# Output parts added in DRAM by accumulating stores from GpSimd, in an attention and gated MLP kernel on one Trainium2 core

## The chip, the cores and the metric

The kernel runs on one core of one Trainium2 chip. Times are device microseconds (us) from the first to the last instruction of an execution on that core, with what lies around it. Smaller is better. The engines are named as the profile names them: PE (TensorE matmul), PEld (its weight load), DVE (VectorE), ACT (ScalarE), POOL (GpSimd) and SP (SyncE, which only issues DMAs here).

## What is computed

Attention over 4 batches, 8 heads, 768 positions and 64 columns a head, where each query sees the first 8 keys and the last 96, with a bias by distance; then a gated MLP over the 3072 tokens, without a nonlinearity:

```python
scores = scale * np.matmul(q, k.transpose(0, 1, 3, 2)) + bias
scores = np.where(keep, scores, -1000000000.0)
a = np.exp(scores - np.max(scores, axis=-1, keepdims=True))
a = a / (np.sum(a, axis=-1, keepdims=True) + 1e-09)
x = np.matmul(a, v)                 # then (tokens, 512)
out = (x @ w_a) * (x @ w_b) @ w_out # 512 -> 1536 -> 512
```

All inputs and the output are float32.

## The kernel before

**Tiling.** The 3072 tokens are cut into six units `u` of 512 tokens. The 1536 inner columns are cut into six pairs of blocks, called `fp`. Not all weights fit at once, so the MLP runs in 18 passes (`PASSES`): each takes one unit through the one to three `fp` whose weights stand in SBUF at that time (`STAYS`, `TURNS`). So a unit's output, 512 tokens by 512 columns, is a sum over several passes. Most products are made by a seven-product scheme for 2x2 block matrices, in which DVE and ACT form the sums of blocks (`forms`, `convert`, `project`, `seven`). Attention for units 1 to 5 runs between the products of the earlier passes (`attention`, `granule_ops`), and ends in the ninth pass; its transposed tiles go through DRAM.

**Numbers as two parts.** A float32 operand is split in a rounded high part and a rest, so each product takes three matmuls. The matmuls into `acc` (`back`, 512 columns) sum a pass in four PSUM banks; in the late passes `strong_back` sums four quarters of the unit in three banks, each product of 256 columns at L1680.

**What happens at the end of a pass.** Where the next pass belongs to another unit, the unit's sum leaves PSUM. In passes 0 to 9 this is `evict`: four tiles `o` of 128 x 512 from three SBUF buffers. When the unit has no part yet, the bank is copied to `o` (`copy`, on ACT or DVE) and stored to a DRAM tensor of its own (`part`). When it has one, the old part is loaded into `o` ahead of time, DVE adds the bank to it (L1854), and `o` is stored to a new part, or to `out` if the unit is done. In passes 10 to 16 `strong_back` does the same for the four quarters, with the add at L1708. The last pass (unit 2) loads its old part into the tile `X` (`start_end`) and adds there. In all there are 32 loads `o<-part`, 4 loads `X<-part`, 36 stores to `part`, 20 stores from `o` to `out` and 5 from `X`; all are issued by SP at L650 (`dma`), save one last store by ACT.

**The order.** Each step is an `Op` with what it reads and writes. `ORDER` is a written-out list of all 3286 steps, and `ON_SCALAR` lists those that run on ACT where ACT and DVE both could. `Schedule.order` walks the list and each engine gets its instructions in that sequence; an engine never passes a waiting instruction. POOL has little to do: the small `TENSOR_SCALAR` on the softmax sums `sm` (L1133), one for each unit and pair of heads.

```python
for index in ORDER:
    op = self.ops[index]
    ...
    op.engine = "act" if index in ON_SCALAR else "dve"
```

Of the kernel before, what the change touches and what calls it, by code (L numbers as in the profile page):

```python
# [615 lines left out]
class Fast:  # L616
# [30 lines left out]
    def dma(self, due, out, src, reads, writes, nbytes, late=0.0):  # L647
# [3 lines left out]
            reads,  # L651
            writes,
            late=late,
            dma=max(nbytes / 325.0, 340.0),
        )

    def copy(self, due, out, src, n, reads, writes, psum=False):
# [1745 lines left out]
```

## Time and profile before

| | |
|---|---|
| time, median of 3 runs | 683.17 us (681.0 to 683.5) |
| profiled execution: time | 682.1 us |
| profiled execution: span | 680.2 us |
| PE busy | 659.8 us, 97% |
| DVE busy | 628.9 us, 92% |
| ACT busy | 390.8 us, 57% |
| POOL busy | 10.9 us, 2% |
| moved by DMA | 160.65 MB |

Matmuls are pipelined: a 256-column matmul is listed with 282 ns, but the next one starts 119 ns later. So the busy share of PE does not tell whether PE is at its pace; the number of matmuls in a stretch does, where they have one shape. The profiled execution's time is 1.9 us more than its span, and it lies inside the range of the runs.

### The profile page before, as it was taken

What the parts mean: (1) busy time and instruction counts of PE and PEld (TensorE: products, weight loads), DVE (VectorE), ACT (ScalarE), POOL (GpSimd) and SP (SyncE); (2) the same over time, 40 slices, a digit from 0 to 9 for tenths busy, and PEclk for the clock granted to TensorE, in tenths of its full rate; (3) what the DMA queues carried; (4) which work ended last, traced back from release to release, by engine and by line L of the source; (5) the groups of instructions that cost most, each with busy time, mean ns of one, the idle gap of its engine ahead of it and who ended that gap; (6) DMA issues with size and microseconds to landing.
All of it is one profiled execution on the core that took longest, in us unless ns stands there. A gap on an engine that the chain in (4) does not pass through costs nothing.

```text
span 680.2 us, 17612 instructions
## 1 busy us (share of the span) xinstructions
PE 659.8 (97%) x6735; PEld 612.6 (90%) x6735; DVE 628.9 (92%) x1632; ACT 390.8 (57%) x1073; POOL 10.9 (2%) x32
## 2 busy tenths in 40 slices
PE   6989999999999999999999999999999999999996
PEld 5779887879997889998999999999999999999996
DVE  8999998999999899869887989899999999999885
ACT  8999675677785666435546546256565346443310
POOL 1000000000000000000000000000000000000000
PEclk9999999999999999999999999999999999999999
DMA  8889999899999999998788986863634653224413
GB/s 331 294 308 292 319 277 327 295 338 317 306 301 354 300 309 296 298 287 284 231 267 234 272 250 197 258 219 109 209 117 166 203 157 112 94 68 140 135 63 114
DMA packets 81871, 160.65 MB, mean 236 GB/s; under 512 B 8114, under 2 KB 36914, under 8 KB 80114
## 3 DMA queue, kind: packets, MB, share of 16 engines
q1 hardware_dynamic: 81490, 159.22, 73.2%
q8 instruction: 55, 0.90, 0.6%
q14 instruction: 38, 0.31, 0.1%
q10 hardware_dynamic: 288, 0.22, 0.1%
HBM read 106.71 MB, written 52.69 MB: 234 GB/s over the span
## 4 chain that ended last, share of the span: by engine, by line
PE 73%; DVE 9%; DMA 9%; ACT 5%; issue 2%; SPq 1%; POOL 0%; DVEq 0%; ACTq 0%; POOLq 0%
PE al L1428 23%; PE ga L1428 17%; PE acc L1620 11%; PE m_acc L1680 7%; PE m_psS L1680 3%; DMA py<-mir 2%; PE ps L1056 2%; ACT t L1040 2%; DMA mir<-tt 2%; DVE tt L1190 2%; PE ps_al L525 1%; PE m_psA L1680 1%; DMA X<-dx 1%; DMA wr<-wts 1%; DMA px<-mir 1%
## 5 line engine op out<-in xcount | busy, mean ns | idle before, releaser
L1620 PE MATMUL acc<-w_O,hh 128*128 128x512 f32 x320 | 113.5, 402 | 0.5 <-DVE hh L662 0.3
L1428 PE MATMUL al<-xf_T,w_S 128*128 128x256 f32 x720 | 95.8, 282 | 0.7 <-ACT s L660 0.7
L1040 ACT ACTIVATE t<-t,sm 128x168 f32<-128x168 f32 x192 | 81.9, 429 | 18.9 <-DVE sm L1024 18.5
L1428 PEld LDWEIGHTS al<-xf_T,w_S 128*128 128x128 f32 x720 | 90.4, 188 | 2.2 <-ACT s L660 1.1
L1620 PEld LDWEIGHTS acc<-w_O,hh 128*128 128x128 f32 x320 | 60.1, 188 | 14.1 <-DVE hh L662 0.7
L1620 PE MATMUL acc<-w_O,hl 128*128 128x512 f32 x160 | 63.1, 394 | 0.2 <-DVE hl L670 0.2
L660 ACT COPY s<-al 128x512 f32<-128x512 f32 x53 | 30.9, 583 | 38.4 <-PE al L1428 37.3
L1024 DVE CUSTOM_DVE_ANT_0 t<-ps,mask 128x168 f32<-128x168 f32 x160 | 47.9, 326 | 1.4 <-PE ps L1056 1.2
L1160 ACT ACTIVATE t<-t,sm 128x168 f32<-128x168 f32 x116 | 40.5, 425 | 14.0 <-DVE sm L1140 13.9
L1428 PE MATMUL ga<-xf_B,w_S 128*128 128x256 f32 x360 | 48.0, 282 | 0.2 <-DVE w_S L670 0.2
L1428 PE MATMUL al<-xf_B,w_A 128*128 128x256 f32 x360 | 47.7, 282 | 0.2 <-DVE sm L1024 0.2
L1428 PE MATMUL al<-xf_T,w_A 128*128 128x256 f32 x360 | 48.0, 282 | 0.0
L1428 PE MATMUL ga<-xf_T,w_S 128*128 128x256 f32 x360 | 47.9, 282 | 0.0
L1428 PE MATMUL ga<-xf_B,w_A 128*128 128x256 f32 x360 | 47.7, 282 | 0.0
L1428 PEld LDWEIGHTS al<-xf_B,w_A 128*128 128x128 f32 x360 | 45.8, 188 | 2.0 <-issue 0.6
L1539 DVE TENSOR_TENSOR s<-ga,s 128x512 f32<-128x512 f32 x60 | 41.0, 684 | 5.4 <-ACT t L1040 2.5
L1428 PEld LDWEIGHTS ga<-xf_B,w_S 128*128 128x128 f32 x360 | 45.1, 188 | 0.6 <-DVE w_S L670 0.4
L1428 PEld LDWEIGHTS ga<-xf_T,w_S 128*128 128x128 f32 x360 | 45.1, 188 | 0.4
L1428 PEld LDWEIGHTS al<-xf_T,w_A 128*128 128x128 f32 x360 | 45.1, 188 | 0.4
L1428 PEld LDWEIGHTS ga<-xf_B,w_A 128*128 128x128 f32 x360 | 45.1, 188 | 0.3
L1190 DVE STREAM_TRANSPOSE tt<-t 128x512 f32<-128x512 f32 x80 | 40.6, 552 | 3.5 <-ACT t L1160 3.2
L660 ACT COPY sa<-al 128x256 f32<-128x256 f32 x26 | 9.7, 372 | 54.1 <-PE al L1428 52.2
(391 smaller groups left out, 1533.0 us busy)
## 6 DMA issues: line engine op xcount, KB each, us to landing
wr<-wts SPq DMA_DIRECT2D x36, 512.0 KB, 5.8
mir<-tt SPq DMA_DIRECT2D x80, 192.0 KB, 4.1
vt<-vd SPq DMA_DIRECT2D x24, 512.0 KB, 6.3
qk<-qk SPq DMA_DIRECT2D x20, 576.0 KB, 6.5
X<-dx SPq DMA_DIRECT2D x11, 1024.0 KB, 6.1
wl_S<-dw_S SPq DMA_DIRECT2D x36, 256.0 KB, 3.4
part<-o SPq DMA_DIRECT2D x36, 256.0 KB, 4.0
px<-mir SPq DMA_DIRECT2D x20, 448.0 KB, 7.3
```

What stands on the lines that cost most here:

```text
L525: self.main.nc.tensor.matmul(self.banks[s][64 * h : 64 * h + 64, o : o + 64], self.vt[rows, v0 : v0 + 64], src[rows, 2 * s : 2 * s + 2, 2 ...
L660: self.nc.scalar.copy(out(), src())
L1024: lambda e: nc.vector.tensor_tensor_reduce(t[:, i, h], bank[:, c0 : c0 + KW], self.mask[pair][:, h, kind], -0.125, 3.0e38, ALU.add, ALU.mi ...
L1040: lambda e: nc.scalar.activation(t[:, i, h], t[:, i, h], AF.Exp, bias=sm[:, 0, j : j + 1], scale=-1.0, accum_out=sm[:, 1, j : j + 1],),
L1056: nc.tensor.matmul(bank[64 * s : 64 * s + 64, c0 + c : c0 + c + w], qk[rows, q0 + 64 * s : q0 + 64 * s + 64], qk[rows, k0 + k : k0 + k + w ...
L1160: nc.scalar.mul(flat()[:, j], flat()[:, j], sm[:, 3, j : j + 1])
L1190: nc.vector.transpose(dst[:, :, e0 : e0 + n], src[:, :, c0 : c0 + 32 * n].rearrange("p j (e k) -> p j e k", e=n),)
L1428: self.nc.tensor.matmul(bank[:, ab * HT : ab * HT + HT], w[:, a, (2 * ab + c) * P : (2 * ab + c) * P + P], x[:, b, c], start=first, stop=F ...
L1539: lambda e: nc.vector.tensor_tensor(s[:, :], bank[:, :], s[:, :], op=ALU.add),
L1620: self.nc.tensor.matmul(acc[i][:, :], a[:, rows], w[:, b], start=first and f == 0 and k == 0, stop=False, skip_group_check=True,)
L1680: self.nc.tensor.matmul(bank[:, c * HT : c * HT + HT], fa(k, c * P, c * P + P), fb(l), start=first, stop=False, skip_group_check=True,)
```

## The change

A unit's part now lies in the unit's own rows of `out`. Its first part is stored there plainly by SP, as before to `part`. Every later part is copied from PSUM to `o` and added to those rows by a store with `accum_op=ALU.add`, issued by GpSimd (`gather`); nothing is loaded. So 32 loads and 32 adds of DVE go, 32 copies (24 on ACT, 8 on DVE) and 32 accumulating stores on POOL come. The last pass still loads its part, now from `out`. The list `ORDER` is new from start to end (3254 steps), and so is `ON_SCALAR`; the planner's other numbers stay.

```diff
 ORDER = (
-    161, 0, 12, 17, 1, 11, 19, 15, 21, 2, 6, 5, 3, 13, 16, 18, 4, 24, 181, 26, 22, 28, 7, 171,
...
+    def gather(self, due, out, src, reads, writes, nbytes):
+        self.plan.op(
+            due,
+            lambda e: self.nc.gpsimd.dma_start(out(), src(), accum_op=ALU.add),
+            reads,
+            writes,
+            dma=nbytes / 325.0,
+        )
...
     def part_of(self, u, due):
-        d = self.dram([NH, P, 512], F32, f"part{u}_{due:.0f}")
-        return d
+        rows = self.out[u * T : u * T + T].rearrange("(a p) c -> a p c", p=P)
+        return self.plan.buf(None, None, F32, f"part{u}", f"part{u}", tile=rows)
...
-        new = None if last or end else self.part_of(u, due)
+        more = old is not None and not end
+        new = None if end else old if more else self.part_of(u, due)
+        if more:
+            old = None
...
-            self.dma(due + n * step, to, at, keys, writes, 512 * 4 * P)
+            (self.gather if more else self.dma)(due + n * step, to, at, keys, writes, 512 * 4 * P)
...
     def evict(self, u, due, acc, first, last, final):
-        new = None if last or final else self.part_of(u, due)
+        old = self.part.get(u)
+        into = not (first or final)
+        new = None if final else old if into else self.part_of(u, due)
...
-                self.plan.op(
-                    due,
-                    lambda e, i=i, o=o: self.nc.vector.tensor_tensor(
-                        o[:, :], acc[i][:, :], o[:, :], op=ALU.add
-                    ),
...
+            self.copy(
+                due, lambda o=o: o[:, :], lambda i=i: acc[i][:, :], 512, [acc[i]], [o], psum=True
+            )
+            (self.gather if into else self.dma)(
```

In the rows of instructions below, a name ends in a running number, and `[waits ...]` names the semaphores of other engines: `DMASW0` to `DMASW7` are those of the accumulating stores, in turn, `DMAHW` those of the DMAs from SP. Most lines of the changed kernel have a number 7 to 10 higher than before (L660 is L667, L1620 is L1627).

POOL, from the softmax of unit 3 to that of unit 5, before:

```order
L1133 TENSOR_SCALAR sm_2_3470<-sm_2_3470 128x8 [waits Activation_49]
L1133 TENSOR_SCALAR sm_3_3871<-sm_3_3871 128x8 [waits Activation_49]
L1133 TENSOR_SCALAR sm_0_4176<-sm_0_4176 128x8 [waits Activation_49,Pool_49]
L1133 TENSOR_SCALAR sm_1_4427<-sm_1_4427 128x8 [waits DVE_49,Activation_49,Pool_49]
L1133 TENSOR_SCALAR sm_2_4702<-sm_2_4702 128x8 [waits DVE_49,Activation_49]
```

and in the changed kernel, where `o_..._232684` are the four tiles with which unit 0 leaves PSUM for the last time (after pass 4) and `o_..._270431` those of unit 1 (after pass 5):

```order
L1140 TENSOR_SCALAR sm_3_3859<-sm_3_3859 128x8 [waits Activation_49,Pool_49]
L658 DMA out<-o_0_232684_4029 128x512 [waits DMAHW7_49,Activation_49]
L658 DMA out<-o_2_232684_4091 128x512 [waits DMAHW2_49,Activation_49]
L1140 TENSOR_SCALAR sm_0_4165<-sm_0_4165 128x8 [waits DVE_49,Activation_49,Pool_49]
L658 DMA out<-o_3_232684_4161 128x512 [waits DMAHW0_49]
L658 DMA out<-o_1_232684_4063 128x512 [waits DMAHW7_49]
L658 DMA out<-o_1_270431_4536 128x512 [waits DMAHW3_49,DVE_49]
L658 DMA out<-o_2_270431_4423 128x512 [waits DMAHW3_49,Activation_49]
L1140 TENSOR_SCALAR sm_1_4406<-sm_1_4406 128x8 [waits Activation_49,Pool_49]
L658 DMA out<-o_0_270431_4544 128x512 [waits DMAHW4_49,DVE_49]
L658 DMA out<-o_3_270431_4691 128x512 [waits DMAHW4_49,Activation_49]
L1140 TENSOR_SCALAR sm_2_4680<-sm_2_4680 128x8 [waits Activation_49,Pool_49]
```

Eight stores have come between five small softmax steps; the other 24 stand behind the last of these, alone.

ACT at the end of the last pass of unit 0, before; here the four adds of this evict are on DVE and ACT has none of them:

```order
L1040 ACTIVATE t3_3_3870,sm3_3_3871<-t3_3_3870,sm3_3_3871 128x168 [waits DVE_49]
L660 COPY s5_3_1_3993<-al5_3_3899 128x512 [waits PE_49]
L660 CAST xf2_T1_248008_3999<-xT1_2_248008_3952 128x512 [waits PE_49]
L1160 ACTIVATE t3_3_3870<-t3_3_3870,sm3_3_3871 128x168 [waits DVE_49,Activation_49]
L1160 ACTIVATE t3_3_3870<-t3_3_3870,sm3_3_3871 128x168 x7
L660 CAST xf2_B11_248008_4051<-X_61 128x512 [waits DMAHW3_49]
L660 COPY sa5_3_4066<-al5_3_3899 128x256 [waits DVE_49,PE_49]
L660 CAST xf2_T4_248008_4072<-xT4_2_248008_4070 128x512 [waits DVE_49]
```

and in the changed kernel (`acc3_0` to `acc3_3` are the four banks of the pass that ends, `al6` is a bank of the next pass):

```order
L667 COPY o0_0_232684_4029<-acc3_0_3167 128x512 [waits DMAHW3_49,PE_49]
L1167 ACTIVATE t3_3_3858<-t3_3_3858,sm3_3_3859 128x168 [waits DVE_49,Activation_49]
L1167 ACTIVATE t3_3_3858<-t3_3_3858,sm3_3_3859 128x168 x3
L667 COPY sa5_3_4049<-al5_3_3877 128x256 [waits PE_49]
L667 COPY o0_1_232684_4063<-acc3_1_3121 128x512 [waits DMAHW4_49,PE_49]
L667 CAST xf2_T4_248008_4070<-xT4_2_248008_4037 128x512
L667 COPY o0_2_232684_4091<-acc3_2_3210 128x512 [waits DMASW0_49,PE_49,Activation_49]
L667 COPY o0_3_232684_4161<-acc3_3_3218 128x512 [waits DMAHW4_49]
L1047 ACTIVATE t4_0_4164,sm4_0_4165<-t4_0_4164,sm4_0_4165 128x168 [waits DVE_49,Pool_49]
L667 COPY vt3_2_3912<-ps4_0_ga_4123 128x4x64 [waits DMAHW2_49,DMAHW1_49,DVE_49]
L667 COPY s6_4_0_4200<-al6_4_4183 128x512 [waits PE_49]
```

All four copies are on ACT now. With three buffers for four tiles, the copy to `o0_2` reuses the buffer of `o0_0`, and waits for the first accumulating store to land (`DMASW0`); the copy to `o0_3` and the copy out of the bank `al6` stand behind it.

## Rows read from the trace of the kernel before

**Rows 1.** The page's first part: busy us, share of the span, instructions.

```profile
PE 659.8 (97%) x6735; PEld 612.6 (90%) x6735; DVE 628.9 (92%) x1632; ACT 390.8 (57%) x1073; POOL 10.9 (2%) x32
```

**Rows 2.** Six stretches: length, busy us (instructions) of each engine, granted clock, DMA, GB/s.

```profile
0.00:120.00 120.00, 107.51 (x1340) 92.50 (x1341) 112.86 (x370) 97.87 (x300) 6.09 (x17) 1.00 0.93 305
120.00:242.00 122.00, 120.53 (x1223) 104.92 (x1221) 117.73 (x297) 85.85 (x227) 1.93 (x6) 1.00 0.96 316
242.00:300.00 58.00, 57.66 (x674) 53.26 (x675) 50.76 (x141) 31.51 (x99) 1.11 (x3) 1.00 0.95 296
300.00:440.00 140.00, 140.00 (x1530) 128.90 (x1529) 123.60 (x321) 72.66 (x216) 1.78 (x7) 1.00 0.83 253
440.00:660.00 220.00, 219.96 (x1857) 219.03 (x1856) 212.71 (x490) 101.35 (x230) 0.00 (x0) 1.00 0.43 139
660.00:680.20 20.20, 14.15 (x120) 13.95 (x118) 11.29 (x19) 1.51 (x3) 0.00 (x0) 0.95 0.33 107
```

**Rows 3.** What PE waited for, 0 to 242 us: us, times, longest.

```profile
PE pu L1242 <- ACT py L660: 2.9, 2, 2.1
PE bank L2230 <- DVE X L2227: 2.4, 1, 2.4
PE ps L1056 <- DMA qk<-qf: 1.7, 1, 1.7
...
```

**Rows 4.** The same view from 242 us to the end.

```profile
PE al L1428 <- ACT s L660: 0.7, 1, 0.7
```

**Rows 5.** Pieces of the chain that ended last: start us, us, what.

```profile
112.08 1.78 PE pa L525 x64
...
259.86 1.44 PE al L1428 x12
...
268.40 2.78 PE acc L1620 x12
```

**Rows 6.** Timeline of PE, one block of score matmuls: start us, us, what.

```profile
251.05 1.11 PE L1056 MATMUL ps<-qk 64*64 64x168 f32 x36
```

**Rows 7.** Groups of DVE by line: form, count, busy us, mean ns, idle before.

```profile
L1024 DVE CUSTOM_DVE_ANT_0 t<-ps,mask 128x168 f32<-128x168 f32 x160 | 47.9, 326 | 1.4 <-PE ps L1056 1.2
L670 DVE TENSOR_TENSOR h<-s 128x256 f32<-128x256 f32 x90 | 36.7, 418 | 0.4
L1708 DVE TENSOR_TENSOR o<-m_acc,o 128x512 f32<-128x512 f32 x27 | 18.3, 684 | 1.0 <-PE m_acc L1680 1.0
L1162 DVE TENSOR_TENSOR t<-t,sm 128x672 f32<-128x672 f32 x11 | 9.3, 851 | 0.4
L1854 DVE TENSOR_TENSOR o<-acc,o 128x512 f32<-128x512 f32 x12 | 8.1, 679 | 1.1 <-PE acc L1620 1.1
L662 DVE CAST xf_T<-xT 128x512 fp32r<-128x512 f32 x9 | 3.8, 421 | 0.0
L662 DVE COPY o<-acc 128x512 f32<-128x512 f32 x4 | 2.7, 686 | 0.3 <-PE acc L1620 0.3
```

**Rows 8.** Tile o: copies on ACT, ns min/median/max, first and last start.

```profile
L660 ACT COPY o<-acc x12: 563/584/594, 117.4 to 418.5; 128x512 f32<-128x512 f32 x12
```

**Rows 9.** DMAs issued from 245 to 300 us: count, KB, median us to landing.

```profile
o<-part SPq DMA_DIRECT2D x8, 256.0 KB, 5.4
...
out<-o SPq DMA_DIRECT2D x5, 256.0 KB, 5.1
...
part<-o SPq DMA_DIRECT2D x1, 256.0 KB, 8.0
```

**Rows 10.** The same view from 440 to 660 us.

```profile
o<-part SPq DMA_DIRECT2D x21, 256.0 KB, 2.8
part<-o SPq DMA_DIRECT2D x20, 256.0 KB, 3.1
```

**Rows 11.** Tile sm on POOL: ns min/median/max; below, who waited for it (us, times).

```profile
L1133 POOL TENSOR_SCALAR sm<-sm x24: 231/312/1030, 11.0 to 423.3; 128x8 f32<-128x8 f32 x24
...
  DVE sm L1140: 1.8, 2
```

More of the change, by code (lines that the diff above doesn't have):

```diff
@@ L1744, in leave @@
                 return
-            if last or end:
+            if end:
                 to = lambda: self.out[r0 : r0 + 2 * P, c0 : c0 + HT].rearrange("(a p) c -> p a c", p=P)
@@ L1837, in evict @@
             o = self.sbuf([P, 512], F32, "o", f"o{u}_{i}_{due:.0f}", 3)
-            if first:
-                self.copy(
-                    due, lambda o=o: o[:, :], lambda i=i: acc[i][:, :], 512, [acc[i]], [o], psum=True
-                )
-            else:
-                old = self.part[u]
-                self.dma(
-                    due - LEADS[4],
-                    lambda o=o: o[:, :],
-                    lambda i=i, old=old: old[i],
-                    [(old, (i, 0)), (old, (i, 1))],
-                    [o],
-                    512 * 4 * P,
-                )
-                self.plan.op(
-                    due,
-                    lambda e, i=i, o=o: self.nc.vector.tensor_tensor(
-                        o[:, :], acc[i][:, :], o[:, :], op=ALU.add
-                    ),
-                    [acc[i]],
-                    [o],
-                    dve=dve(512),
-                )
-            if last:
-                r = u * T + i * P
-                self.dma(
-                    due, lambda r=r: self.out[r : r + P], lambda o=o: o[:, :], [o], [], 512 * 4 * P
-                )
-            else:
-                self.dma(
-                    due,
-                    lambda i=i: new[i],
-                    lambda o=o: o[:, :],
-                    [o],
-                    [(new, (i, 0)), (new, (i, 1))],
-                    512 * 4 * P,
-                )
+            self.copy(
+                due, lambda o=o: o[:, :], lambda i=i: acc[i][:, :], 512, [acc[i]], [o], psum=True
+            )
+            (self.gather if into else self.dma)(
+                due,
+                lambda i=i: new[i],
+                lambda o=o: o[:, :],
+                [o],
+                [(new, (i, 0)), (new, (i, 1))],
+                512 * 4 * P,
+            )
         if new:
```

479 rows, old and new, of tables (ON_SCALAR, ORDER) are left out of this document.

## The prediction

> **What bounds the kernel now.** I read the busy shares first [rows 1]: PE 97%, DVE 92%, everything else far below. A busy PE is not yet a PE at its pace, so the next views are the stretches [rows 2] and the list of what PE waited for [rows 3, 4]. They cut the run in two. Up to 242 us PE waits in many small pieces for ACT, DVE and a DMA; the sixteen rows of that list, of which three are shown, add up to 13.3 us [rows 3], and PE is busy 107.5 of the first 120 us [rows 2]. DVE is at work 112.9 of 120 and 117.7 of 122 us there [rows 2]: this part goes at DVE's pace. After 242 us PE waits once, for 0.7 us [rows 4], and is busy 417.6 of 418 us up to 660 [rows 2]. That this is a full pace is shown by the chain: twelve matmuls of 256 columns take 1.44 us, 120 ns each, twelve of 512 take 2.78 us, 232 ns each [rows 5], and from 440 to 660 us 1857 matmuls, almost all of 256 columns, make 118 ns each [rows 2]. The granted clock is 1.00 throughout, its upper level of 2.4 GHz, and 0.95 only in the last stretch, when PE has run dry [rows 2]. The last 6 us are a tail of adds and stores that the change leaves as it is.
>
> So from 242 us on, work that DVE or the DMA queues are spared is work beside a full PE, and is worth nothing by itself. What can move the time is PE's waits before 242 us, and new waits after.
>
> **The change part by part.**
>
> *The loads.* 32 loads of 256 KB leave SP's queue. The first was issued at 251 us, behind the border, so each lies beside a full PE: 0. While DMA is 0.95 busy up to 300 us, the loads made room for no one that PE waited for [rows 2, 4]. Gone with them is the add's wait for its load; late next is the copy's wait for its buffer, below.
>
> *The adds.* 12 adds at L1854 of 679 ns and 20 of those at L1708 of 684 ns go: 21.8 us of DVE [rows 7]. 32 copies come: 8 on DVE of 686 ns, 5.5 us [rows 7], 24 on ACT of 584 ns, 14.0 us [rows 8]. The new list also moves other steps between the two. Counted by form over the whole program, DVE has 32 512-column two-input steps fewer, and more: 2 copies (686), 7 casts (421), 16 casts half as wide (at most 421), 4 multiplies at L1162 (851), 3 half copies (about 418) [rows 7]. That is 21.8 less 1.4, 2.9, 3.4 to 6.7, 3.4 and 1.3, so DVE does 6 to 9 us less. All adds stood after 242 us: 0 on the path. If PE were not full there, it would be up to these 9 us.
>
> *The new list before 242 us.* This part has no accumulating store and no missing load; only the order differs. I compare both orders at one step that both have, just behind the border: the first matmul that reads the second half of the output weights of `fp` 3 (`w3_O1`), whose last writer is a DVE instruction. Before it DVE has 4 more 512-column two-input steps (684), 2 more of 256 (418), 2 more masked steps of L1024 (326), 2 more at L1162 (851) and one copy less (686): 2.74 + 0.84 + 0.65 + 1.70 - 0.69 = 5.2 us [rows 7]; the other differences are small copies that cancel. PE has 36 more 256-column matmuls done by then, 36 x 120 ns = 4.3 us that it need not do later [rows 5]. If DVE sets the time of this step, the change is 5.2 - 4.3 = +0.9 us; if PE does, 0. I take +0.5, since the trace has both near their pace here. How well the new list fills DVE's own gaps (7.1 and 4.3 us idle in the two stretches) no order tells; see the second rival.
>
> *The accumulating stores.* 32 on POOL, which is busy 10.9 us in all [rows 1] and whose queue holds only the 24 small softmax steps [rows 11]. Eight stores stand among these; each softmax step behind a store is fed by activations that ACT runs after the copy that the store waits for, so nothing is held back. The cost is in landing. A copy into `o` that reuses a buffer waits for the store that empties it, and in the copy's queue PSUM copies wait behind it, for which PE waits. The tightest place is the end of unit 0. From the last matmul into `acc3_0` to the first of the next pass into the bank of `acc3_2`, PE has 24 matmuls of 256 columns (2.9 us), 21 of 512 (4.9), 24 score matmuls (24/36 of 1.11) and 32 value matmuls (32/64 of 1.78): 2.88 + 4.87 + 0.74 + 0.89 = 9.4 us [rows 5, 6]. Two copies of 0.58 us [rows 8] must fit, so the first store has 8.2 us from the end of the copy to landing, POOL's issue included. The next is the end of unit 1: 48 matmuls of 256 and 12 of 512 and the same attention block, 5.76 + 2.78 + 1.63 = 10.2 us, less a copy on DVE and one on ACT, 8.9 us. In the late passes, the closest pairs I find in the order leave 10 us and more.
>
> How long such a store takes, no row shows. It moves 256 KB and also has to read its target. The near ends are a plain store, 5.1 us in this stretch (5.4 a load, 8.0 the slowest row) and a load and a store one after the other, 10.5 [rows 9]; the far end is two of the slowest, 16.0. After 440 us it is 3.1 to 5.9 [rows 10], under the 10 us that it has. At 5.1 to 8.0 it costs nothing, at 10.5 it costs 2.3 + 1.6 = 3.9 us, at 16.0 7.8 + 7.1 = 14.9. I take no cost: one transfer that reads and writes as it goes is nearer to one store than to two in turn. A gain is excluded, since PE waits for no store now [rows 3, 4]. The page "DMA: Bandwidth & Descriptors" of the Trainium skill (section "Anatomy of one DMA — SWDGE (gpsimd) path") fits such a GpSimd-issued DMA as 2.0 us plus its bytes at 436 GB/s, an estimate of 2.6 us here without the accumulation; by that the cost is also nothing, and the sum stays.
>
> *The sum.* 682.1 (the profiled execution) + 0 + 0 + 0.5 + 0 = 682.6 us. The median of the runs stands 1.1 above the profiled time and the lowest run 1.1 below it; I take 683.0.
>
> **The rivals.**
>
> *A, slower: the landing takes PE's banks.* The place is the buffer of `o0_0`, and the point from which it decides is a landing of 8.2 us. DMA is 0.95 busy there [rows 2], which speaks for it, and the slowest plain store already took 8.0 [rows 9]; against it, a queue of its own does not stand behind SP's backlog. At 10.5 us it gives 683.0 + 3.9 = 686.9. For this rival speaks a rule of the Trainium skill, page "SBUF — State Buffer", section "SBUF: two separate sides": GpSimd writes the descriptors of its DMAs through a port that it shares with DVE, and cannot while DVE runs certain fast steps, such as copies and casts within SBUF, so the DMA starts late. The trace shows something like it: one softmax step on POOL took 1030 ns where the median is 312 [rows 11]; that is 0.7 us of the 8.2, and would not decide alone.
>
> *B, faster: the new list fills the waits before 242 us.* DVE is idle 11.4 us there, PE waits 13.3 [rows 2, 3]. For it: the start is where all loss is, and every row of the list is new. Against it: at the common step both orders have the same work ahead within a microsecond. Half of DVE's idle time is 5.7 us, so 683.0 - 5.7 = 677.3.
>
> *C, slower: DVE becomes the bound late.* From 440 to 660 us DVE is idle 7.3 of 220 us [rows 2], and 20 stores are issued there. If each held up DVE for POOL's longest step, 1.03 us [rows 11], it would be 20.6 us, against 7.3 idle and the 20 adds that go there less 4 copies that come on DVE, 13.7 - 2.7 = 11.0 [rows 7]: 20.6 - 7.3 - 11.0 = +2.3, so 685.3. Against it: in the whole run DVE waited 1.8 us for POOL's 24 steps, 1.03 us at most for one [rows 11].
>
> **How the numbers follow.** The forecast, same pace and no landing wait, has 0.45 (683.0, from 680 to 686); A 0.20 (686.9, up to 697.9); B 0.24 (677.3); C 0.06 (685.3); other ends of a wholly new order 0.05, slower. A measurement of this kernel tells about 0.5% from no change, 3.4 us, so "same" is 679.8 to 686.6. Faster is B: 0.24. Slower is A, half of C and the rest: 0.28. Same is the forecast and the other half of C: 0.48. The range reaches down to 676, a little beyond B, and up to 690, which is A with a landing of 12 us; I leave 0.08 below it and 0.10 above.
>
> **What would show it.** Right: after about 245 us PE has no row of waits over 1 us, DVE's total falls by 6 to 9 us, ACT's rises, no load `o<-part` is left, and the accumulating stores land within 8 us. A shows as ACT idle before a copy to `o` near 255 to 262 us with the DMA `out<-o` named, and PE waiting for ACT behind it. B shows as PE busy over 110 of the first 120 us. C shows as longer DVE steps while POOL issues. The forecast is wrong if PE waits anywhere late, or if the first 242 us of work end more than 3 us earlier or later than now.

## The result, and the profile after

The changed kernel takes 685.42 us (median of ten runs, 683.07 to 690.49); the kernel before, timed beside it, takes 681.45 (ten runs, 680.19 to 683.5). The ratio is 1.0062, with an interval of 1.0038 to 1.0086. Three later comparisons of the same kernel gave 1.0034, 1.0050 and 1.0058; the mean of the four is 1.0051, which is 3.5 us. So the time that came lies 2.4 us above the forecast of 683.0 and inside the range, but "the same" was wrong: the kernel is slower, by about half a per cent. The profiled execution took 685.42 us, its span is 683.6; before it was 682.1 and 680.2.

The page's first part and its queues, after (for the first line, compare [rows 1]; a queue's line has packets, MB and share of the 16 DMA engines):

```profile
PE 660.2 (97%) x6735; PEld 613.0 (90%) x6735; DVE 623.7 (91%) x1630; ACT 391.7 (57%) x1063; POOL 44.4 (7%) x64
...
q1 hardware_dynamic: 67154, 142.44, 66.4%
q0 software_dynamic: 7168, 8.39, 9.2%
```

PE's work is the same to 0.4 us, and DVE did give up 5.2 us. POOL's busy time quadrupled: each store costs it about a microsecond of issuing ((44.4 - 10.9) / 32). The 8.39 MB of the 32 stores are cut into 7168 packets.

The same stretches as in [rows 2] (length, then busy us and instructions of PE, PEld, DVE, ACT, POOL, then granted clock, DMA share, GB/s):

```profile
0.00:120.00 120.00, 107.13 (x1338) 92.16 (x1339) 110.78 (x364) 99.99 (x308) 5.54 (x17) 1.00 0.94 302
120.00:242.00 122.00, 119.49 (x1223) 105.19 (x1222) 119.53 (x302) 84.36 (x227) 1.40 (x5) 1.00 0.97 314
242.00:300.00 58.00, 56.78 (x668) 51.94 (x667) 49.24 (x131) 27.38 (x81) 4.41 (x7) 1.00 0.97 268
300.00:440.00 140.00, 139.80 (x1528) 128.75 (x1527) 120.22 (x316) 74.98 (x220) 5.58 (x11) 1.00 0.82 242
440.00:660.00 220.00, 219.68 (x1840) 217.84 (x1839) 210.35 (x497) 101.94 (x222) 23.12 (x21) 1.00 0.49 118
660.00:684.00 24.00, 17.33 (x147) 17.13 (x145) 13.54 (x25) 3.07 (x7) 4.37 (x4) 0.94 0.53 92
```

PE is no longer full in the third stretch (56.78 of 58 us, 57.66 before). From 440 to 660 us it does 17 instructions fewer than before, but that is no sign of a slower pace: this execution comes to 440 us later in its work, and `after_again`, a second profile of the same kernel (experiment 2), has 1855 in the same window. The DMA share there rose from 0.43 to 0.49 (0.47 and 0.48 in the other profiles of this kernel; 0.36 and 0.37 in the SP kernel below, whose stores are plain), though the loads are gone: 20 adding stores keep the DMA engines busy for longer than the loads and plain stores that they replace.

What PE waited for from 242 us to the end, after; before it was one wait for 0.7 us [rows 4]:

```profile
PE acc L1627 <- ACT o L667: 1.4, 2, 1.2
PE ga L1435 <- DVE s L1546: 0.2, 1, 0.2
```

The 1.2 us is the wait that rival A names. ACT's timeline shows it (start us, us, what; in brackets the idle time before, and what ended it):

```profile
268.69 0.62 ACT L667 CAST xf_T<-xT 128x512 fp32r<-128x512 f32 x1
275.27 1.08 ACT L667 COPY o<-acc 128x512 f32<-128x512 f32 x2 [5.96 <-DMA out<-o]
```

and so does the chain of work that ended last, from 265 us on (start us, us, what):

```profile
265.12 10.05 DMA out<-o
...
275.27 0.59 ACT o L667
...
275.90 1.66 PE acc L1627 x6
```

The store was issued at 265.12 us and landed 10.05 us later. The prediction gave it 8.2 us. ACT stood before its copy for 5.96 us, with the next copy behind it; PE lost 1.2 us of that. But 1.2 us are not 3.5, and the other three profiles of this kernel have less: their waits of PE for ACT's copies to `o` add up to 0.3, 0.7 and 0.8 us. Most of the loss is not in the list of waits at all.

To find it I compared traces of the same list of instructions. The matmuls then come in the same order, so the time between the starts of two numbered matmuls can be set side by side. Four profiles of the changed kernel stand here against two of a kernel (`sp_plain` and `sp_again`, below) that has the same list and the same transfers, with every one of the 32 stores a plain store on SP's queue:

| matmuls | about when, us | stores on GpSimd, adding: mean (lowest to highest) | all on SP, plain | difference |
|---|---|---|---|---|
| 1 to 2250 | 2 to 214 | 210.6 (209.58 to 211.50) | 210.2 | +0.4 |
| 2250 to 2500 | 214 to 235 | 22.26 (20.73 to 24.60) | 20.81 | +1.45 |
| 2750 to 3000 | 257 to 281, end of unit 0 | 23.34 (22.90 to 24.33) | 23.20 (22.93 and 23.46) | +0.14 |
| 3250 to 3500 | 304 to 326, end of unit 1 | 22.75 (22.49 to 23.05) | 22.25 | +0.50 |
| 3500 to 5500 | 326 to 529 | 202.99 | 202.99 | 0 |
| 5500 to 6000 | 529 to 590 | 60.31 (60.13 to 60.44) | 59.87 | +0.44 |
| 6000 to 6734 | 590 to 677 | 87.51 | 87.52 | 0 |
| last matmul to the end | | 6.53 (6.50 to 6.57) | 5.65 | +0.89 |

The stretches from 2500 to 2750 and from 3000 to 3250, left out of the table, differ by 0.02 us or less in the mean. From 304 us on, the means of stretches in which nothing differs agree to 0.02 us, and the ranges of the three that differ do not overlap: 0.50, 0.44 and 0.89 us are clear of the noise. The 0.14 us at the end of unit 0 are not, since the two columns overlap there; nor are the first 0.4 us. The 1.45 us at 214 to 235 us stand before the first adding store is issued.

### The profile page after: what moved, and what is told of

The parts are those of the page before. It is cut to its first block, busy times and chain, and to the rows that moved or that the text cites. A ratio compares the mean times of both kernels' runs of the same rounds, so it can differ in the third digit from the quotient of the medians.

```text
span 683.6 us, 17567 instructions
## 1 busy us (share of the span) xinstructions
PE 660.2 (97%) x6735; PEld 613.0 (90%) x6735; DVE 623.7 (91%) x1630; ACT 391.7 (57%) x1063; POOL 44.4 (7%) x64
## 3 DMA queue, kind: packets, MB, share of 16 engines
q0 software_dynamic: 7168, 8.39, 9.2%
## 4 chain that ended last, share of the span: by engine, by line
PE 50%; DVE 13%; DMA 8%; issue 4%; ACT 2%; POOL 0%; SPq 0%; DVEq 0%; ACTq 0%; POOLq 0%
PE al L1435 18%; PE ga L1435 13%; PE acc L1627 7%; PE m_acc L1690 5%; DMA out<-o 3%; PE m_psS L1690 2%; DMA dx<-vt 2%; DMA px<-mir 1%; DVE h L677 1%; DVE s L1546 1%; DMA dw_S<-wm 1%; PE m_psA L1690 1%; DMA wr<-wts 1%; PE ps L1063 1%; DVE tt L1197 1%
## 5 line engine op out<-in xcount | busy, mean ns | idle before, releaser
L1627 PE MATMUL acc<-w_O,hh 128*128 128x512 f32 x320 | 114.0, 401 | 2.5 <-ACT o L667 1.4
L1047 ACT ACTIVATE t<-t,sm 128x168 f32<-128x168 f32 x192 | 81.9, 429 | 12.2 <-DVE sm L1031 11.8
L1627 PEld LDWEIGHTS acc<-w_O,hh 128*128 128x128 f32 x320 | 60.1, 188 | 15.4 <-ACT o L667 1.7
L1627 PE MATMUL acc<-w_O,hl 128*128 128x512 f32 x160 | 63.0, 394 | 0.0
L667 ACT COPY s<-al 128x512 f32<-128x512 f32 x54 | 31.5, 584 | 40.2 <-PE al L1435 36.4
L658 POOL DMA_DIRECT2D out<-o x32 | 34.8, 1109 | 248.6 <-DVE o L1718 121.7
L1167 ACT ACTIVATE t<-t,sm 128x168 f32<-128x168 f32 x100 | 35.0, 424 | 13.5 <-DVE sm L1147 13.5
```

The costliest lines, as they stand in the source:

```text
L658: lambda e: self.nc.gpsimd.dma_start(out(), src(), accum_op=ALU.add),
L667: self.nc.scalar.copy(out(), src())
L1047: lambda e: nc.scalar.activation(t[:, i, h], t[:, i, h], AF.Exp, bias=sm[:, 0, j : j + 1], scale=-1.0, accum_out=sm[:, 1, j : j + 1],),
L1167: nc.scalar.mul(flat()[:, j], flat()[:, j], sm[:, 3, j : j + 1])
L1627: self.nc.tensor.matmul(acc[i][:, :], a[:, rows], w[:, b], start=first and f == 0 and k == 0, stop=False, skip_group_check=True,)
```

## The experiments

Unless something else is said, the edit is to the changed kernel. Ratios are to the kernel before, timed beside each run.

**1. Where the accumulation and GpSimd come in.** Two kernels keep the new list and all its transfers. One issues the 32 stores on GpSimd without adding; the other moves them to SP:

```diff
-            lambda e: self.nc.gpsimd.dma_start(out(), src(), accum_op=ALU.add),
+            lambda e: self.nc.gpsimd.dma_start(out(), src()),      # pool_plain
+            lambda e: self.nc.sync.dma_start(out(), src()),        # sp_plain, sp_again
```

> The changed kernel with its 32 accumulating stores as plain stores from the same queue (the addition in DRAM is left out, so the parts overwrite each other). Theory L, if it is the addition that is slow: the first store at the end of unit 0 lands in about 5 us, ACT's wait of 6 us and PE's waits of 1.2 and 0.2 us go: 684 us, ratio 1.004. Theory O, or if the GpSimd queue is slow whatever it carries: 685.4 us, ratio 1.006.

> The changed kernel with its 32 accumulating stores as plain stores in SP's queue at the same places of the list (the addition in DRAM is left out). Theory L: landing near the 5 us of the plain stores, no PE wait at the end of unit 0: 684 us or less, ratio 1.003 to 1.004; what pool_plain loses against this is the GpSimd queue. Theory O: 685.4 us, ratio 1.006.

Measured: `sp_plain` 682.22 us, 1.0004 (0.9984 to 1.0023), and the same kernel once more 1.0005 (0.9985 to 1.0025). `pool_plain` 684.11 us, 1.0043 (1.0020 to 1.0065). So the new list with its copies and without the loads costs nothing that can be measured, and the loss goes when the stores are plain and on SP. In these kernels the parts overwrite each other instead of being added. Dropping the addition alone does not return it. The queue lines of `pool_plain`:

```profile
q0 software_dynamic: 2560, 8.39, 3.4%
```

The same bytes take 2560 packets and a third of the DMA time that the adding stores took, 3.4% against 9.2%. The places agree with this in part. At the end of unit 1 `pool_plain` needs the 22.25 us of the SP kernel, so the +0.50 there belongs to the addition. From 529 to 590 us it needs 60.38, so that loss stays with GpSimd, whether its stores add or not. Its tail is 6.35, but its last output store lands as early as on SP, 4.1 us behind the start of the last matmul; what is longer stands behind that landing, and one profile does not tell why. So 0.5 of the 2.7 us by which `pool_plain` is slower than `sp_plain` (1.0043 less 1.0004) are placed. Its one profile, a long execution with a span of 688.0 us, has large losses before 242 us (near 82 us and from 214 to 235), which experiment 4 and the last of the points below take up.

> The changed kernel with all 32 accumulating stores as plain stores in SP's queue, once more (the addition in DRAM is left out). If the stores on GpSimd are the loss: 1.000 to 1.001 again, and few executions above 683.5 us. If the new list is the loss and the first result was luck: 1.003 to 1.005.

The repeat of the SP kernel was run beside a repeat of the changed kernel, and gave the second column of the table its second profile.

**2. The new kernel again.** Three times, for the spread and for profiles to average:

> The changed kernel once more, for a second look at where its 4 us go and as a control beside the next runs. Theory L (the landing of the accumulating stores): the first one, at the end of unit 0, takes about 10 us again, ACT stands about 6 us before the copy to o, PE waits 1 to 2 us there. Theory O (the new list alone): the same ratio of 1.006 to the kernel before, whatever the landing does; PE's loss is spread in small waits before 242 us and after 540 us.

> The changed kernel a third time, as the control beside the two others: 683.5 to 685.5 us, ratio 1.003 to 1.006; a third look at the landing of the first accumulating store (10.0 us in the first two looks) and at PE's wait for px and py near 82 us (1.8 and 0 us).

> The changed kernel as the control: 683.5 to 685.5 us, ratio 1.003 to 1.006.

1.0034 (1.0016 to 1.0052), 1.0050 (1.0024 to 1.0075), 1.0058 (1.0033 to 1.0083). The landing that decides at each of the two tight places is that of the first store there. Beside it stands the time of the stretch of 250 matmuls around it:

| profile | first store of unit 0: landing | matmuls 2750 to 3000 | first store of unit 1: landing | matmuls 3250 to 3500 |
|---|---|---|---|---|
| changed kernel | 10.05 | 24.33 | 8.81 | 22.49 |
| `after_again` | 7.59 | 22.93 | 8.88 | 22.59 |
| `after_third` | 8.04 | 22.90 | 9.34 | 23.05 |
| `after_fourth` | 8.89 | 23.19 | 9.16 | 22.88 |
| `pool_plain` | 6.23 | 22.91 | 7.90 | 22.25 |
| `sp_plain` | 9.01 | 23.46 | 5.08 | 22.25 |
| `sp_again` | 8.25 | 22.93 | 5.80 | 22.25 |

So the expectation's "10.0 us in the first two looks" holds for the first look alone; the second had 7.59. At the end of unit 0 the stretch grows with a landing over some 8.5 us, whatever the store is, and adding stores (7.6 to 10.05) are not shown to land later than plain ones on SP (8.25 and 9.01). At the end of unit 1 they are: 8.8 to 9.3 us against 7.90 and less, and from 8.55 us on each 0.1 us of landing costs PE 0.1 us.

**3. The list.** `old_order` has the list of before, with each add turned into a copy on ACT and the loads taken out; its stores add. `old_order_sp` is the same with plain stores on SP.

```diff
 ORDER = (
-    (the new list)
+    (the list of before, without its 32 loads; 24 of the copies on ACT)
```

> The accumulating stores and the copies, in the list of the kernel before: each copy stands where the add stood, each accumulating store where the store stood, the loads are left out; the same 24 copies are on ACT as in the changed kernel. Theory L: the stores land as late as in the changed kernel, ACT waits for a buffer of o at the end of unit 0 and PE behind it: 683 to 686 us, ratio 1.003 to 1.006. Theory O: without the new list nothing is lost: 681 to 682 us, ratio 0.999 to 1.001.

> The list of the kernel before, copies for adds, no loads, and all 32 stores plain in SP's queue (the addition in DRAM is left out). If the stores on GpSimd are the loss: the 1.0083 of the same list with accumulating stores falls to 0.999 to 1.001. If it is the copies on ACT in places made for adds on DVE: it stays at 1.004 or more.

Measured: 1.0083 (1.0053 to 1.0112) and 1.0034 (1.0022 to 1.0047). So with plain stores the old list costs 0.3% where the new one costs nothing: its places for adds are the wrong ones for copies. Against the kernel before, the stretch of matmuls 2750 to 3000 takes 24.65 instead of 23.25 us, and that of 6250 to 6500 30.91 instead of 29.72. The new order is therefore no side matter: it takes back what the copies cost. With adding stores the tail grows from 5.98 to 8.35 us. POOL's timeline at the end of `old_order` shows how (start us, us, what, idle before and what ended it):

```profile
667.53 1.22 POOL L659 DMA_DIRECT2D out<-o  x1 [6.88 <-DVE o L1719]
672.13 1.20 POOL L659 DMA_DIRECT2D out<-o  x1 [3.39 <-issue]
677.64 1.21 POOL L659 DMA_DIRECT2D out<-o  x1 [4.31 <-DVE X L1730]
```

The tiles of the first two were both ready by 667.1 us, but the second store leaves 4.6 us after the first. The third, whose tile was ready at 677.09, leaves 0.3 us after the landing of the second and lands at 682.97 us, 5.33 us after its issue and after the rest of the program; as a plain store on SP it takes 2.60 us.

**4. Is the loss in the first 120 us?** A profile of the changed kernel and that of `pool_plain` had a matmul waiting near 82 us for a load (`px`, `py`), and that suggested a theory: the early order, not the stores, costs the time.

> The changed kernel, but its first 1226 steps (up to about 190 us, where both lists have done the same steps but for two each) stand in the order and on the engines of the kernel before; from there on the new list. Theory E (the new list's start: a load of px and py that lands 8 to 11 us after its issue, for which PE waits 0 to 2.9 us near 82 us, longer in slow runs): the loss goes, 681 to 682.5 us, ratio 0.999 to 1.001. Theory G (the GpSimd queue of the stores, wherever they land): 683.5 to 684.5 us, ratio 1.003 to 1.005, as in the changed kernel.

> The mirror image: the kernel before, with its loads and adds and no accumulating store, but its first 1226 steps in the order and on the engines of the new list. Theory E: 683 to 684.5 us, ratio 1.002 to 1.005, with a PE wait near 82 us for a DMA. Theory G: 681 to 682 us, ratio 0.999 to 1.001.

`early_old` has the first 1226 of the list's 3254 steps in the order of before, `before_early_new` is the kernel before with its first 1226 steps in the new order. Measured: 1.0045 (1.0028 to 1.0062) and 1.0016 (0.9995 to 1.0037). The old start does not cure the new kernel, and the new start does not spoil the old one by an amount that can be told. The theory fell. A second attempt moved the load instead, ahead of two weight loads of 512 KB in SP's queue:

```diff
 (SP's queue)
-L698 DMA wr_3<-wts 128x512
-L698 DMA wr_4<-wts 128x512
 L648 DMA px<-mir_1 112x1024
 L648 DMA py<-mir_1 64x512 x2
+L698 DMA wr_3<-wts 128x512
+L698 DMA wr_4<-wts 128x512
```

> The changed kernel with one edit of the list: two 512 KB weight loads that stand in SP's queue just ahead of the loads of px and py (the first value matmul after 82 us waits for these, up to 2.9 us, and in the run with the longest wait the granted clock fell to 0.89 behind it) stand just behind them. Theory E (that wait is what sets the changed kernel's slow executions): px and py land 2 to 3 us sooner, the wait goes, 682 to 683 us, ratio 1.001 to 1.002, and few executions above 684. Theory G (the stores on GpSimd): as the changed kernel, 683.5 to 684.5 us.

> The changed kernel with the loads of px and py ahead of two weight loads, and all 32 stores plain in SP's queue (the addition in DRAM is left out). If both the list and the GpSimd stores cost: 0.997 to 1.000. If only the GpSimd stores cost: as the kernel with all stores on SP, 1.000 to 1.001. If only the list costs: 1.002, as with the accumulating stores.

Measured: 1.0021 (1.0005 to 1.0037) with the adding stores, 1.0015 (0.9993 to 1.0037) with all stores on SP. The first looked like a cure for half of the loss. The second shows no gain from the move when the stores are plain, and a later kernel with the same move (experiment 6) gained nothing by it. I don't count it as a cause.

What the wait does to the clock can be seen in `pool_plain`, in two stretches around 82 us:

```profile
80.00:85.00 5.00, 3.04 (x25) 2.83 (x23) 4.88 (x12) 4.04 (x9) 0.02 (x1) 1.00 1.01 284
85.00:100.00 15.00, 14.05 (x170) 12.31 (x171) 10.13 (x33) 9.85 (x31) 0.23 (x1) 0.89 0.83 257
```

PE was busy for 3.04 of 5 us, and in the 15 us after that the granted clock was 0.89: part of that time at the lower of its two levels, 1.2 GHz instead of 2.4. The 250 matmuls that hold the wait take 18.94 us there (15.53 and 16.22 in the SP kernel), and the next 250 take 24.82 (23.92 and 23.80). That may be the price of the lower clock, but it isn't shown: `loads_first_sp` has no such wait and a clock of 1.00 there, and takes 24.66.

**5. Which stores.** `sp_12` puts the 12 stores of the first passes on SP, plain, and leaves 20 adding stores late; `sp_late20` does the opposite.

```diff
-            (self.gather if into else self.dma)(
+            self.dma(                                              # sp_12
...
-            (self.gather if more else self.dma)(due + n * step, to, at, keys, writes, 512 * 4 * P)
+            self.dma(due + n * step, to, at, keys, writes, 512 * 4 * P)  # sp_late20
```

> The changed kernel with 12 of its 32 accumulating stores (those at the ends of units 0, 1 and 2, before 450 us, while DMA is busy) as plain stores in SP's queue (their addition is left out), the 20 late ones as they are. Theory E: 683.5 to 684.5 us, ratio 1.003 to 1.005, as the early list is the same. Theory G: where the loss is the landing under a busy DMA, 682 us and a ratio of 1.000 to 1.001, as with all 32 on SP; where it is the late stores, 683.5 to 684.5 us.

> The mirror of the kernel with 12 stores on SP: the 12 accumulating stores at the ends of units 0 to 2 stay, the 20 of the late passes are plain stores in SP's queue (their addition is left out). If the late stores carry the loss (they go out one at a time, each 0.3 us after the one before has landed, and the last one lands beside the last output stores): the tail behind the last matmul falls from 6.5 to 5.7 us, PE gains 0.3 to 0.5 us between 440 and 660 us, 682 to 683 us, ratio 1.001 to 1.002. If the landings at the ends of the units carry it: ACT's wait of up to 6 us and PE's of up to 1.2 us stay, 683.5 to 684.5 us, ratio 1.003 to 1.005.

Measured: 1.0034 (1.0018 to 1.0051) and 1.0050 (1.0031 to 1.0068). This doesn't add up to the 1.0051 of both together, so the ratios give no split. The stretches do better, at two places: `sp_12` has 22.25 at the end of unit 1, with its own 12 stores plain, and 60.29 from 529 to 590, where its adding stores are; `sp_late20` has 59.82 there, and 22.57 at the end of unit 1, where its stores add. Each place follows the stores that stand at it. This holds in the other kernels too: with the early stores adding, the end of unit 1 takes 22.36 to 23.13 us in all nine profiles that have the new list there, and 22.25 in the five with plain ones. The late stretch hangs on the list as well: under the old list of experiment 3 it takes 59.95 us with adding stores and 59.99 without. The tail does not follow the stores: 6.15 in `sp_12`, but 8.44 in `sp_late20`, whose late stores are plain; its last transfer landed at 681.73 us and its span ended at 686.0. I have one profile of it and no explanation. For the +1.45 before the first store see the points below.

**6. The one-at-a-time issue.** An adding store of the late passes (L1761) writes two blocks of 128 rows. In POOL's timeline of the changed kernel the last ones stand in a regular row:

```profile
649.72 1.19 POOL L658 DMA_DIRECT2D out<-o  x1 [10.59 <-DVE o L1718]
654.62 1.21 POOL L658 DMA_DIRECT2D out<-o  x1 [3.70 <-issue]
659.57 1.19 POOL L658 DMA_DIRECT2D out<-o  x1 [3.75 <-issue]
...
669.46 1.19 POOL L658 DMA_DIRECT2D out<-o  x1 [3.94 <-ACT o L667]
674.26 1.20 POOL L658 DMA_DIRECT2D out<-o  x1 [3.60 <-DVE X L1867]
```

and the view of the tile gives the landing of the one of 654.62 (ns of its issue, when, and us to landing):

```profile
L658 POOL DMA_DIRECT2D out<-o x1: 1209/1209/1209, 654.6 to 654.6; - x1
...
DMA to landing us min/median/max: 4.6/4.6/4.6
```

654.62 + 4.6 = 659.2, and the next is issued at 659.57: some 0.3 us after the landing, and so on down the row. In none of the four profiles of this kernel are two of these 20 stores under way together. The program has no such wait. The last store is held until 674.26 and lands at 678.97, among the final stores of the output; on SP the three last of these stores went out at 660.6 to 666.3 us (in `sp_again`, whose end comes 3 us sooner). To test whether the size of one store is what limits it, `halves` issues each as two of 128 rows:

```diff
+    def pieces(self, out, src):
+        if len(src.shape) < 3:
+            return [(out, src)]
+        return [(out[:, k], src[:, k]) for k in range(2)]
...
-            lambda e: self.nc.gpsimd.dma_start(out(), src(), accum_op=ALU.add),
+            lambda e: [
+                self.nc.gpsimd.dma_start(to, at, accum_op=ALU.add)
+                for to, at in self.pieces(out(), src())
+            ],
```

`halves_loads` has the moved loads of experiment 4 as well.

> The changed kernel with each of the 20 late accumulating stores cut into two (128 rows of 1 KB each, where one store had 256). If the size of a store keeps the next one from being issued: a second store goes out while the first is under way, the queue no longer falls 4.7 us per store behind, the tail behind the last matmul falls from 6.5 to 5.7 to 6.1 us, and PE's two stretches near 500 to 590 us lose 0.4 us; 682.5 to 685 us, ratio 1.002 to 1.004. If an accumulating store always waits for the one before it: tail 6.5 us or more, ratio 1.004 to 1.006.

> The same with the loads of px and py ahead of two weight loads, near 72 us. If both edits take away what they are meant to: 681.5 to 683 us, ratio 1.000 to 1.002, no slower than before. If not: 683 to 685 us, 1.002 to 1.005.

Measured: 683.78 us, 1.0030 (1.0014 to 1.0046), and 683.86, 1.0031 (1.0016 to 1.0046). POOL's timeline of `halves`:

```profile
648.62 2.66 POOL L664 DMA_DIRECT2D out<-o  x3 [10.00 <-DVE o L1726]
651.80 0.86 POOL L664 DMA_DIRECT2D out<-o  x1 [0.52 <-issue]
652.94 0.86 POOL L664 DMA_DIRECT2D out<-o  x1 [0.28 <-issue]
654.11 0.99 POOL L664 DMA_DIRECT2D out<-o  x1 [0.31 <-issue]
```

The row of 3.6 us gaps is gone: gaps are 0.3 to 0.5 us, and the tail falls from 6.53 to 5.96, by 0.6 of the 0.9 us. So the issue does depend on the size of a store. There is still a bound: the first three of this row leave together, the fourth leaves 0.31 us after the landing of the first (648.62 us + 2.87), and so on; of the 40 half stores never more than three are under way, and 11 leave 0.31 us after the landing of the third before them. The packets tell a likely reason:

```profile
q0 software_dynamic: 7488, 8.39, 9.4%
```

A half store has 144 packets and a whole one 272 (12 x 144 + 20 x 272 = 7168; 52 x 144 = 7488). Three halves are 432 packets and may go together, two whole ones would be 544 and do not. A bound on packets under way, somewhere between, would fit both kernels, and also `pool_plain`, whose stores have 80 each and leave three together; no run tests it.

The price turns up elsewhere. PE's waits from 500 to 660 us in `halves`:

```profile
PE ga L1443 <- ACT s L675: 0.9, 1, 0.9
PE ga L1443 <- DVE s L1554: 0.3, 1, 0.3
```

Two stores side by side near 550 us hold up a load of SP's, ACT's weights behind it, and PE; the stretch of matmuls 5500 to 6000 takes 61.14 us. On the clock `halves` stands below the mean of the changed kernel, but its interval reaches over the 1.0034 of `after_again`, so a gain isn't shown. A fourth buffer of `o` was not tried.

**7. The kernel before once more**, for a trace against which the stretches can be checked:

> The kernel before once more, unchanged: a second look at how far its stretches differ between two executions. All theories: 680 to 684 us; from 450 us on within 0.3 us of the first look, before that within 2 us.

682.34 us. After 450 us its stretches agree with those of the first trace to 0.3 us, with one exception of 0.8 us (matmuls 5250 to 5500, 30.81 against 29.99), which was not expected. A single stretch of one profile can thus be off by nearly a microsecond; the means of the table above, whose ranges don't overlap at 304 to 326 us, 529 to 590 us and in the tail, are safer.

No kernel of these beats the kernel before.

## Why the prediction was off, point by point

**Loads, adds, list: right.** The all-SP kernel has the new list, no loads and the copies, and takes 1.0004 and 1.0005 of the time before, 0.3 us; the sum had +0.5 for these. DVE fell by 5.2 us (628.9 to 623.7; 6 to 9 were forecast), ACT rose by 0.9, and neither moved the time. This fits the reason given, that from 242 us on PE is full and spared work is worth nothing: without its loads and adds the SP kernel is no faster. Experiment 3 adds what the prediction did not weigh: the same edit under the old list would have cost 0.3%.

**Rival B did not happen.** PE is busy 107.13 of the first 120 us, 107.51 before; B asked for over 110.

**The step that failed is the price of the adding stores: "I take no cost: one transfer that reads and writes as it goes is nearer to one store than to two in turn".** In its place the four comparisons showed 3.5 us, of which 0.5 us stand at the end of unit 1, 0.44 in the late passes and about 0.5 in the tail; the rest stays open. At the end of unit 1 the first adding store landed in 8.8 to 9.3 us, where plain ones took 7.90 on GpSimd and 5.1 to 5.8 on SP. The two ends worked out from [rows 9] were 5.1 us (one store) and 10.5 (a load and a store in turn): it is nearer to the upper one, which I had called the less likely. In the late passes it takes 4.4 us in the median (4.0 to 6.8, 80 stores in four profiles) for the same 256 KB, against 3.1 of a plain store and 5.9 of a load and a store in turn [rows 10]: halfway between. On this the Trainium skill, page "DMA: Bandwidth & Descriptors" (section "Anatomy of one DMA — SWDGE (gpsimd) path"), agrees for the store that does not add: its fit gives an estimate of 2.6 us, and the 20 late plain stores of `pool_plain` took 2.6 us in the median (2.5 to 5.8). The adding stores took 1.7 times that in the median of the late passes, and up to 3.9 times in the first profile at the end of unit 0 (10.05 us).

A second part of the error is the place itself: at the end of unit 0 even a plain store on SP took longer than the 5.1 us. The view of the tile in `sp_again`, at the same step:

```profile
L658 SPq DMA_DIRECT2D out<-o x1: 557/557/557, 264.9 to 264.9; - x1
...
  ACT o L667: 3.4, 1
DMA to landing us min/median/max: 8.3/8.3/8.3
```

8.3 us, with ACT waiting 3.4 us and PE not at all. Rival A was priced at 3.9 us for a landing of 10.5 at both places; 0.64 us came on the mean, 0.14 at unit 0, which is not clear of the noise, and 0.50 at unit 1. The budgets were fair: the forecast was 8.2 and 8.9 us, and by the table of experiment 2 the stretches begin to grow at some 8.5 us in both places. The landings are what lay lower, 7.6 to 10.05 us. So A named the right mechanism, but its sure place is the end of unit 1, and it is a seventh of the loss.

**The tail.** The prediction called it "a tail of adds and stores that the change leaves as it is". Against the kernel before that is nearly so: 6.36 and 6.27 us in its two profiles, 6.53 after. But the same list with plain stores on SP ends in 5.65, so what the list had won is lost. The prediction looked at the last stores only for their landing time (under the 10 us they have) and not for when they can be issued. They go out one at a time, the last one lands among the final stores of the output, and the last of these lands 4.45 to 4.79 us behind the start of the last matmul, where the SP kernel has 4.1; in `halves` it is 4.1 again. That is 0.5 of the 0.89 us. The other 0.4 us stand behind the last landing, a time that is 1.4 to 2.3 us in these kernels, with adding stores and without (4.3 in `sp_late20`), and I don't put it down to the stores.

**The late passes were called free, and cost 0.44 us.** The prediction weighed who waits for an adding store, and there it was right: no such wait is in PE's list. It did not weigh what the store's transfers do to others. Matmul by matmul the difference stands at two places: 0.04 to 0.34 us between numbers 5720 and 5740, and 0.14 between 5900 and 5920, where PE waits 0.2 us for DVE. DMA issues from 530 to 590 us, after:

```profile
out<-o POOLq DMA_DIRECT2D x8, 256.0 KB, 4.6
...
wl_A<-dw_A SPq DMA_DIRECT2D x4, 256.0 KB, 4.4
```

and with the same stores plain on SP (`sp_again`; the last number is the median us to landing):

```profile
out<-o SPq DMA_DIRECT2D x8, 256.0 KB, 3.6
...
wl_A<-dw_A SPq DMA_DIRECT2D x4, 256.0 KB, 2.9
```

SP's loads of `wl_A`, which are not part of the change, take 4.4 us instead of 2.9. ACT waits for them after, and has no such row in `sp_again` (us, times, longest):

```profile
ACT w_A L667 <- DMA wl_A<-dw_A: 1.4, 2, 1.0
```

The chain of the changed kernel has one of these loads in it, the only transfer there between 437 and 660 us:

```profile
550.13 5.24 DMA wl_A<-dw_A
```

It starts 21 us behind matmul 5500; the load at the same step takes 5.2 to 5.4 us in all four profiles, and the loss at 5720 is least, 0.04 us, where ACT waits least (1.0 us). `sp_late20`, with plain stores on SP there, has 59.82 us for the stretch, like `sp_again`. In `pool_plain`, whose stores are plain, the load at this step takes 4.92 us and the one just before it 5.49, ACT waits 1.8 us for `w_A`, and the stretch is as long as with adding stores. So it is not the addition that does it here, but stores that go out in a queue of their own, beside SP's loads instead of in line with them.

**Rival C did not happen.** DVE's steps are as long as before, though POOL issues between them: 682 ns against 684 for a 512-column step, 325 against 326 for the masked one [rows 7]. The groups of DVE, after (form, count, then busy us and mean ns):

```profile
L1031 DVE CUSTOM_DVE_ANT_0 t<-ps,mask 128x168 f32<-128x168 f32 x160 | 47.5, 325 | 2.5 <-PE ps L1063 2.3
...
L1718 DVE TENSOR_TENSOR o<-m_acc,o 128x512 f32<-128x512 f32 x15 | 10.2, 682 | 0.0
```

**Open: the 1.45 us before the first adding store.** Matmuls 2250 to 2500 take 20.73 to 24.60 us in kernels whose later stores are issued on GpSimd and 20.72 to 20.91 in three profiles with all on SP. No store has been issued on GpSimd by then, and of the ten profiles with stores on GpSimd six lie at 20.73 to 21.50 and four at 22.97 to 24.60. Where it is long, PE had waited: in the fourth profile of the changed kernel,

```profile
222.00:232.00 10.00, 7.00 (x127) 5.74 (x126) 8.70 (x25) 7.65 (x25) 0.23 (x1) 0.90 0.74 253
232.00:240.00 8.00, 8.00 (x60) 7.81 (x60) 6.37 (x14) 5.69 (x13) 0.00 (x0) 0.91 0.48 164
```

PE was busy 7.00 of 10 us with the granted clock at 0.90, and the 8 us behind it were granted 0.91; `sp_again` was busy 8.81 of the same 10 us at 1.00. Such a loss needs no store on GpSimd: `before_early_new`, which has none, takes 23.03 us there, where the kernel before takes 21.35 and 21.33. And four of the 24 timed runs of the SP kernel took 685.4 to 686.8 us, so it has long executions too, of which none was profiled. With three profiles on one side I can't say whether the stores have a part in it or whether it is chance. The medians of the timed runs differ by 3.2 us between the changed kernel and the SP one; some 1.4 us are shown to be at the stores' places (0.5 at unit 1, 0.44 late, 0.5 in the tail), and the other 1.8 us stay open.

## What to carry to other kernels

A transfer that becomes cheaper for the engines can become dearer for the queues: before a load and a store are merged into an adding store, compare its own landing time with the time that its buffer has, and reckon with up to the sum of load and store as its price until a trace shows another. Then look at who shares the DMA engines at that time: a load in another queue that lands 1.5 us later is a wait nobody changed in the code. Take that from more than one profile, and from the same steps of the list, not from the same window of time. When the change touches no engine at its limit, compare stretches between numbered matmuls of the same list; a loss of half a microsecond here and there, which no list of waits shows, stands out there.

## What the runs showed of the hardware

- An accumulating DMA of 256 KB from GpSimd takes 4.4 us in the median of the late passes (four profiles), a plain one from GpSimd 2.6 (`pool_plain`). At the end of unit 1, where the DMA engines have no room (share 1.06 from 303 to 315 us), it is 8.8 to 9.3 us for the first store, against 7.9. At the end of unit 0 no difference from plain stores on SP is shown (7.6 to 10.05 against 8.25 and 9.01). The 32 stores move the same bytes in 7168 instead of 2560 packets and keep the DMA engines busy 9.2% of the span instead of 3.4%.
- Adding stores of 256 rows (two blocks of 128) leave GpSimd only when the one before has landed, some 0.3 us behind it. Of half stores of 128 rows up to three are under way, and the next leaves 0.3 us after the landing of the third before it. A bound on packets (over 432, under 544) would explain both; no run tests it.
- Stores in GpSimd's queue, adding or plain, run beside SP's loads: at one step near 550 us a 256 KB load of `wl_A` took 5.2 to 5.4 us beside adding ones and 4.9 beside plain ones, and the load just before it 4.4 to 4.7 and 5.5, where it took 2.9 and 3.0 with all stores on SP.
- GpSimd itself is busy about a microsecond for each store; DVE's steps grew no longer by it.
